# Four of seven products of a tile take the high and the low half of the weights in one matmul of 512 columns, and both late operands are made before the second product begins

## The chip, the cores and the metric

The kernel runs on one core of a Trainium2 chip. The time is device microseconds (us) of one execution, the median of three: 558.22 (557.73 to 558.32). Five engines run side by side, each with a queue of its own that is worked off in order: PE (TensorE, matmuls; its weight loads are shown as PEld), DVE (VectorE), ACT (ScalarE), POOL (GpSimd) and SP (here it issues DMAs). They wait for each other by semaphores.

## The reference, cut to what matters

```python
attn_out = _attn_ref(**attn_kwargs)              # causal softmax attention mixed with a memory read
x = attn_out.transpose(0, 2, 1, 3).reshape(2304, 512)
h = x @ w_in                                      # w_in 512 x 2048: the first product
r = np.maximum(h, 0.0)
g = s * (r * r) + b
return g @ w_out                                  # w_out 2048 x 512: the second product
```

## The kernel before

Until about 287 us the kernel computes attention, with most of the first product in its gaps. The rest of the first product runs to 373 us; beside it the weights `w_out` are loaded and made ready. The second product takes the rest. Everything in float32 is kept as two halves, H (rounded to fp32r) and L = x - H; a product of two such numbers is H\*BH + H\*BL + L\*BH, three matmuls into one PSUM tile.

The second product works on nine tiles of 256 rows (`t`). A tile is a 2 x 2 block of matrices a11, a12, a21, a22, and Winograd's scheme makes of eight block products seven, numbered 1 to 7 in `m`. Their operands are single blocks or sums of blocks; on the side of `w_out` the sums are made once (`t_u`, `split_u`, `late_b`), on the side of g for every tile (`operand`). A product has 1024 rows to sum over, eight steps `f`; its operand comes in two pieces `c` (four steps each). `SEQ` gives the order of the products in a tile, and operands are made two products ahead (`AH`), in eight buffers `xs`, so for four products. The operand's H is made by a cast on ACT (line 738), its L by a subtraction on DVE, or on POOL for products 1, 2 and 4 (line 739). The sums of blocks are made on DVE for products 5 and 6 (lines 735 and 737), on POOL for 7 and 3 (line 733). In the text, "6c1" is the second piece of product 6.

ACT also turns r into g for the next tile, in four pieces of four blocks each, a Square (line 712) and a scale with bias (line 713); `g_load` fetches the pieces from DRAM, into `w0L` and `w1L` in turn. `combine` adds the products into the output: one ACT copy (line 757) and seven DVE additions with one source in PSUM (lines 759 to 770) for a tile. PSUM tiles of a product are 128 x 256, eight of them.

Products 4 and 2 use the last weights to be ready, the "late" ones: H is cast from `late32` while the first product ends (line 682), L is subtracted on DVE in the first four products of tile 0 (line 684), since its place `w1H` is in use until the first product's last matmul.

A scheduler in the framework orders the queues by its own timeline, except where `pin` keeps an instruction in the program's order; so the order on an engine is not that of the code.

Of the kernel before, what the change touches and what calls it, by code (L numbers as in the profile page):

```python
# [165 lines left out]
def attention_moe_kernel(  # L166
# [456 lines left out]
    PL = {m: n for n, m in enumerate((1, 3, 5, 6, 7))}  # L623
    w2 = ctx.enter_context(tc.tile_pool(name="w2", bufs=1, side="right", reuse_waits="tile"))
    bHs, bLs = {}, {}
    RAW = [0, 1, 2, 3, 4, 5, 6, 7, 4, 5, 6, 7, 8, 6, 7, 8]
    NRAW = 4
    NEXT = {n: (n + 4,) for n in range(9)} | {3: (), 4: (7, 8)} | {10: (13,), 11: (14,), 12: (15,)}

    def load_u(n):  # L630

        t = w2.tile([128, DM, 2], U32, tag=f"row{RAW[n]}", name="raw")
        r = n // 2 + n % 2 * KF
        nc.sync.dma_start(t, words(w_out)[128 * r:128 * r + 128])
        st["u", n] = t

    def stage(i):

        if i == 0:
            return stg0  # L640
        if i < 4:
            k = 4 + 2 * ((i + 1) % 2)
            return [w2.tile([128, 4, NE], F32, tag=f"bl{k + j}", name="stg1") for j in range(2)]
        return stg[2 * (i % 2)], stg[2 * (i % 2) + 1]

    def conv_u(n):
        i, h = divmod(n, 2)
        if h == 0:
            st["b"] = stage(i)
        w, s = st["b"]  # L650
        conv64(st.pop(("u", n)), w[:, 2 * h:2 * h + 2].rearrange("p a b -> p (a b)"))
        if n in NEXT:
            for r in NEXT[n]:
                load_u(r)
        if h == 0:
            return
        later(2, t_u, i, w, s)
        later(4, split_u, i, w, s)

    def t_u(i, w, s):  # L660

        b12, b21, b22 = w[:, 1], w[:, 2], w[:, 3]
        t1, t2, t3 = s[:, 0], s[:, 1], s[:, 2]
        nc.vector.tensor_sub(t1, b12, w[:, 0])
        nc.vector.tensor_sub(t3, b22, b12)
        nc.vector.tensor_sub(t2, b22, t1)
        nc.vector.tensor_sub(late32[:, i, 0], t2, b21)

    def split_u(i, w, s):
        pin(nc.scalar.copy(late32[:, i, 1], w[:, 2]))  # L670
        bHs[i] = w2.tile([128, 5, NE], F32R, tag=f"row{i}", name="bH")
        bLs[i] = w2.tile([128, 5, NE], F32R, tag=f"bl{i}", name="bL")
        for x, a, n in ((w[:, 0:1], 0, 1), (w[:, 3:4], 1, 1), (s[:, 0:3], 2, 3)):
            L, H = bLs[i][:, a:a + n], bHs[i][:, a:a + n]
            pin(nc.scalar.copy(H, x))
            nc.vector.tensor_sub(L, x, H.bitcast(F32))

    def late_b(n, part):

        hs = slice(KF // 4 * n, KF // 4 * n + KF // 4)  # L680
        if part == 0:
            nc.scalar.copy(late[0][:, hs], late32[:, hs])
        else:
            nc.vector.tensor_sub(late[1][:, hs], late32[:, hs], late[0][:, hs].bitcast(F32))

    def b_op(m, f):
        if m in LATE:
            return [t[:, f, LATE.index(m)] for t in late]
        return bHs[f][:, PL[m]], bLs[f][:, PL[m]]

    NPT = NT // 256
# [25 lines left out]
    def operand(t, m, c):  # L717

        r = SRC[t % 2]
        f1 = slice(4 * c, 4 * c + 4)  # L720
        f2 = slice(KF + 4 * c, KF + 4 * c + 4)
        A = {11: r[:, f1, 0:128], 12: r[:, f2, 0:128], 21: r[:, f1, 128:256], 22: r[:, f2, 128:256]}
        if m == 7 and not SUM:
            both = w2.tile([128, 2, 4, 128], F32, tag="row8", name="sum")
            SUM.extend(both[:, i] for i in range(2))
        o = xpool.tile([128, 2, 4, 128], F32R, tag="xs", name="op")
        OPS[t, m, c] = o
        H, L = o[:, 0], o[:, 1]
        x = A[{1: 11, 7: 11, 5: 21, 6: 11, 3: 12, 2: 12, 4: 22}[m]]
        if m in (7, 3):  # L730
            y = x
            x = SUM[c]
            nc.gpsimd.tensor_sub(x, y, A[{7: 21, 3: 11}[m]])  # L733
        elif m == 5:
            nc.vector.tensor_add(x, x, A[22])
        elif m == 6:
            nc.vector.tensor_sub(x, A[21], x)  # L737
        nc.scalar.copy(H, x)  # L738
        (nc.gpsimd if m in ONPOOL else nc.vector).tensor_sub(L, x, H.bitcast(F32))  # L739

    def product(t, m):
        ps = ps_y.tile([128, NE], F32, tag="y", name="yps")
        for f in range(KF):
            o = OPS[t, m, f // 4]
            H, L = o[:, 0, f % 4], o[:, 1, f % 4]
            BH, BL = b_op(m, f)
            nc.tensor.matmul(ps, lhsT=H, rhs=BH, start=f == 0, stop=False)  # L747
# [24 lines left out]

    ONPOOL = (1, 2, 4)
# [9 lines left out]
    stg0 = [w2.tile([128, 4, NE], F32, tag=f"row{i}", name="stg0") for i in (8, 7)]
    for i in range(4, 7):
        w2.tile([128, 5, NE], F32, tag=f"row{i}", name="row")
    late32 = w2.tile([128, KF, 2, NE], F32, tag="late", name="late32")
    for i in range(KF):
        w2.tile([128, 5, NE], F32, tag=f"bl{i}", name="blr")

    def slot16(tag, dtype):  # L790
        return wpool.tile([128, KF, 2, NE], dtype, tag=tag, name=tag)
# [94 lines left out]
```

## Time and profile before

| | us |
|---|---|
| median of three runs | 558.22 |
| the profiled execution, its own time | 559.67 |
| its span, first to last instruction | 557.8 |
| PE busy | 542.8 |
| ACT busy | 397.4 |
| DVE busy | 359.4 |
| POOL busy | 302.5 |
| second product, first to last matmul start | 373.20 to 553.68 |

The profiled execution has 1.9 us around its span and is 1.45 us above the median. The granted clock of TensorE is 1.0 of full speed in all of the second product. A timeline row gives start and duration; rows of an engine overlap a little, so the pace of an engine is read from start to start. In brackets stands the time for which the engine sat idle before the row, and what ended it.

### The profile page before, as it was taken

How to read it: one execution, taken by the hardware profiler on the slowest of the kernel's cores; microseconds unless marked ns; L12 is line 12 of the kernel's file. 1: busy time of each engine (PE TensorE's matmuls, PEld its weight loads, DVE VectorE, ACT ScalarE, POOL GpSimd, SP SyncE). 2: the span in 40 equal slices, each digit the busy share in tenths (PEclk: the TensorE clock that was granted, in tenths of full speed). 3: DMA queues.
4: the chain of work that ended last, by engine and by line, in shares of the span. 5: the costliest groups of instructions: out<-in, count | busy, mean ns of one | idle time of the engine just before them, and what ended most of it. 6: DMA issues, size and time to landing. Idle time of an engine off the chain costs nothing.

```text
span 557.8 us, 12012 instructions
## 1 busy us (share of the span) xinstructions
PE 542.8 (97%) x4364; PEld 458.7 (82%) x4364; DVE 359.4 (64%) x885; ACT 397.4 (71%) x869; POOL 302.5 (54%) x327
## 2 busy tenths in 40 slices
PE   8997998999999999999999999999999999999997
PEld 6765766776777777777788888899999999999997
DVE  3999988999655554123108878336966786687562
ACT  5999877875968786337326568958779778877940
POOL 2788898768684595202200000325687678768750
PEclk8999899999999999999999999999999999999999
DMA  6546567664344343221137766447444435353101
GB/s 214 160 140 197 154 206 233 198 209 144 115 162 118 127 131 103 85 77 58 58 118 283 260 200 219 139 162 245 145 130 148 147 105 170 105 164 112 39 29 38
DMA packets 56666, 81.52 MB, mean 146 GB/s; under 512 B 7584, under 2 KB 39072, under 8 KB 56608
## 3 DMA queue, kind: packets, MB, share of 16 engines
q1 hardware_dynamic: 53616, 77.94, 43.6%
q10 hardware_dynamic: 2992, 2.82, 1.5%
q8 instruction: 34, 0.56, 0.4%
q14 instruction: 24, 0.20, 0.1%
HBM read 57.15 MB, written 23.59 MB: 145 GB/s over the span
## 4 chain that ended last, share of the span: by engine, by line
PE 80%; DVE 8%; POOL 5%; ACT 3%; issue 2%; DMA 1%; SPq 0%; POOLq 0%; DVEq 0%; ACTq 0%
PE yps L749 9%; PE yps L747 9%; PE yps L748 9%; PE tb L534 8%; PE sb L474 6%; PE tb L535 6%; PE tb L536 6%; PE sb L354 6%; PE hps L534 5%; PE hps L535 5%; PE hps L536 5%; PE tb L431 4%; POOL P L373 3%; DVE P L361 2%; ACT P L367 1%
## 5 line engine op out<-in xcount | busy, mean ns | idle before, releaser
L373 POOL TENSOR_SCALAR P<-P,sr,omg 128x192 f32<-128x192 f32 (+4 forms) x160 | 111.8, 712 | 63.2 <-DVE sr L405 42.7
L749 PE MATMUL yps<-bH,op 128*128 128x256 f32 x360 | 101.5, 282 | 0.7 <-DVE op L739 0.7
L747 PE MATMUL yps<-bH,op 128*128 128x256 f32 x360 | 101.3, 281 | 0.0
L748 PE MATMUL yps<-bL,op 128*128 128x256 f32 x360 | 101.3, 281 | 0.0
L367 ACT ACTIVATE P<-P,mn 128x64 f32<-128x64 f32 (+4 forms) x160 | 88.6, 564 | 13.7 <-DVE mn L361 13.3
L733 POOL TENSOR_TENSOR sum<-w0L 128x512 f32<-128x512 f32 x20 | 30.4, 1518 | 109.4 <-ACT w0L L713 87.9
L361 DVE CUSTOM_DVE_ANT_0 P<-sb,mask 128x64 f32<-128x64 f32 (+4 forms) x160 | 70.0, 482 | 28.8 <-PE sb L354 28.6
L749 PEld LDWEIGHTS yps<-bH,op 128*128 128x128 f32 x360 | 68.0, 189 | 1.0 <-DVE op L739 0.9
L748 PEld LDWEIGHTS yps<-bL,op 128*128 128x128 f32 x360 | 68.0, 189 | 0.0
L747 PEld LDWEIGHTS yps<-bH,op 128*128 128x128 f32 x360 | 67.9, 189 | 0.0
L354 PE MATMUL sb<-qk 64*128 64x288 f32 (+4 forms) x384 | 57.1, 418 | 3.9 <-DVE mn L361 2.6
L431 PEld LDWEIGHTS tb<-ident,P 64*128 64x128 f32 x928 | 37.7, 140 | 17.9 <-POOL P L373 6.8
L354 PEld LDWEIGHTS sb<-qk 64*128 64x128 f32 x384 | 36.4, 191 | 17.0 <-issue 8.6
L431 PE MATMUL tb<-ident,P 64*128 64x64 f32 x928 | 44.2, 231 | 4.2 <-POOL P L373 2.9
L441 ACT COPY pt<-tb 128x512 f32<-128x512 f32 x64 | 34.5, 596 | 18.7 <-PE tb L431 11.5
L739 POOL TENSOR_TENSOR op<-w0L,op 128x512 fp32r<-128x512 f32 x30 | 42.3, 1428 | 4.9 <-ACT op L738 4.7
L555 ACT ACTIVATE r<-tb 128x512 f32<-128x512 f32 x41 | 24.4, 594 | 26.9 <-PE tb L536 19.5
L733 POOL TENSOR_TENSOR sum<-w1L 128x512 f32<-128x512 f32 x16 | 24.4, 1528 | 32.1 <-DVE op L739 28.0
L738 ACT CAST op<-w0L 128x512 fp32r<-128x512 f32 x50 | 30.0, 616 | 16.1 <-DVE w0L L737 8.7
L534 PE MATMUL tb<-xs,w0H 128*128 128x512 f32 x96 | 40.7, 424 | 0.2 <-ACT F L443 0.2
L747 PE MATMUL yps<-w0H,op 128*128 128x256 f32 x144 | 40.8, 283 | 0.0
L748 PE MATMUL yps<-w1H,op 128*128 128x256 f32 x144 | 40.7, 283 | 0.0
(137 smaller groups left out, 1458.9 us busy)
## 6 DMA issues: line engine op xcount, KB each, us to landing
r_d<-r SPq DMA_DIRECT2D x41, 256.0 KB, 2.0
w0L<-r_d SPq DMA_DIRECT2D x20, 512.0 KB, 4.5
qk<-in_qk_t_dram SPq DMA_DIRECT2D x15, 576.0 KB, 4.4
raw<-in_moe_w_out_dram SPq DMA_DIRECT2D x16, 512.0 KB, 5.7
w1L<-r_d SPq DMA_DIRECT2D x16, 512.0 KB, 4.5
xa<-in_moe_w_in_dram SPq DMA_DIRECT2D x12, 512.0 KB, 4.5
r_d<-r SPq DMA_DIRECT2D x48, 128.0 KB, 1.8
qs<-in_q_rows_dram SPq DMA_DIRECT2D x15, 320.0 KB, 3.5
```

The costliest lines, as they stand in the source:

```text
L354: nc.tensor.matmul(SB[ps[j]][:, o:o + n], lhsT=qk[rs, 128 * i:128 * i + 128], rhs=qk[rs, S + 64 + c0:S + 64 + c0 + n], start=True, stop=Tr ...
L361: nc.vector.tensor_tensor_reduce(P[:, j, PB[i] + 64:PB[i] + 64 + n], SB[ps[j]][:, o:o + n], m, -SCALE, 3.0e38, ALU.add, ALU.min, mn[:, j, ...
L367: nc.scalar.activation(pt, pt, AF.Exp, scale=-1.0, bias=mn[:, j, i:i + 1], accum_out=sm[:, j, i, 0:1])
L373: nc.gpsimd.tensor_scalar(pt, pt, sr[:, j, i:i + 1], omg[:, h:h + 1], ALU.mult, ALU.mult)
L431: nc.tensor.transpose(TB[ps[h]][:, o[h]:o[h] + 64], P[rs, j, c:c + 128], ident[rs, rs], tile_position=(64 * h, 0))
L534: nc.tensor.matmul(ps, lhsT=wH[:, p, fs], rhs=xs[:, 0], start=p == 0, stop=False)
L535: nc.tensor.matmul(ps, lhsT=wH[:, p, fs], rhs=xs[:, 1], start=False, stop=False)
L536: nc.tensor.matmul(ps, lhsT=wL[:, p, fs], rhs=xs[:, 0], start=False, stop=p == NP - 1)
L733: nc.gpsimd.tensor_sub(x, y, A[{7: 21, 3: 11}[m]])
L747: nc.tensor.matmul(ps, lhsT=H, rhs=BH, start=f == 0, stop=False)
L748: nc.tensor.matmul(ps, lhsT=H, rhs=BL, start=False, stop=False)
L749: nc.tensor.matmul(ps, lhsT=L, rhs=BH, start=False, stop=f == KF - 1)
```

## The change

In `product`, the weights' H and L of a block now lie side by side (`RB`, and `late` with the same order inside), and products 1, 6, 3 and 2 (`WIDE`) multiply H with both in one matmul of 512 columns into a PSUM tile of 128 x 512, whose two halves are summed later. L\*BH goes into the first half. Products 5, 7 and 4 stay as they were, in half of such a tile. `combine` adds both halves, so it has eleven DVE additions for a tile instead of seven, beside the ACT copy.

The order of products is now 1, 5, 6, 7, 3, 2, 4. Product 5's sum a21 + a22 goes to a buffer of its own, `SUM`; product 6's operand is made in that same buffer, product 7's in place of a21, product 3's again in `SUM`. Before, 5 and 6 were made in place in the tile, and `SUM` held those of 7 and 3. Product 4 has the other sign in its weights.

`late_b` makes H and L together while the first product ends, into what were `w0H` and `w0L`; tile 0's pieces are then loaded where `late32` was, so `first_load` comes after `late_b`, five steps later than before. The rooms in which `w_out` is loaded and staged are cut differently; the work on them is the same.

```diff
-    SEQ = [1, 7, 5, 6, 3, 2, 4]
+    SEQ = [1, 5, 6, 7, 3, 2, 4]
...
-        nc.vector.tensor_sub(late32[:, i, 0], t2, b21)
+        nc.vector.tensor_sub(T32[i // 2][:, i % 2, 0], b21, t2)
...
-    def late_b(n, part):
-
-        hs = slice(KF // 4 * n, KF // 4 * n + KF // 4)
-        if part == 0:
-            nc.scalar.copy(late[0][:, hs], late32[:, hs])
-        else:
-            nc.vector.tensor_sub(late[1][:, hs], late32[:, hs], late[0][:, hs].bitcast(F32))
+    def late_b(n):
+
+        t = late[n // 2][:, 2 * (n % 2):2 * (n % 2) + 2]
+        H, L = t[:, :, :, 0], t[:, :, :, 1]
+        nc.scalar.copy(H, T32[n])
+        nc.vector.tensor_sub(L, T32[n], H.bitcast(F32))
...
-        x = A[{1: 11, 7: 11, 5: 21, 6: 11, 3: 12, 2: 12, 4: 22}[m]]
-        if m in (7, 3):
-            y = x
-            x = SUM[c]
-            nc.gpsimd.tensor_sub(x, y, A[{7: 21, 3: 11}[m]])
-        elif m == 5:
-            nc.vector.tensor_add(x, x, A[22])
+        x = {1: a11, 5: SUM[c], 6: SUM[c], 2: a12, 7: a21, 3: SUM[c], 4: a22}[m]
+        if m == 5:
+            nc.vector.tensor_add(x, a21, a22)
         elif m == 6:
-            nc.vector.tensor_sub(x, A[21], x)
+            nc.vector.tensor_sub(x, x, a11)
+        elif m == 7:
+            nc.gpsimd.tensor_sub(x, a11, x)
+        elif m == 3:
+            nc.gpsimd.tensor_sub(x, a12, x)
         nc.scalar.copy(H, x)
         (nc.gpsimd if m in ONPOOL else nc.vector).tensor_sub(L, x, H.bitcast(F32))
 
+    WIDE = (1, 6, 3, 2)
+
     def product(t, m):
-        ps = ps_y.tile([128, NE], F32, tag="y", name="yps")
+        OPS["ps", m] = tile = ps_y.tile([128, 2, NE], F32, tag="y", name="yps")
+        ps = tile[:, 0]
         for f in range(KF):
             o = OPS[t, m, f // 4]
             H, L = o[:, 0, f % 4], o[:, 1, f % 4]
-            BH, BL = b_op(m, f)
-            nc.tensor.matmul(ps, lhsT=H, rhs=BH, start=f == 0, stop=False)
-            nc.tensor.matmul(ps, lhsT=H, rhs=BL, start=False, stop=False)
-            nc.tensor.matmul(ps, lhsT=L, rhs=BH, start=False, stop=f == KF - 1)
+            B = b_op(m, f)
+            if m in WIDE:
+                nc.tensor.matmul(tile, lhsT=H, rhs=B, start=f == 0, stop=False)
+            else:
+                nc.tensor.matmul(ps, lhsT=H, rhs=B[:, 0], start=f == 0, stop=False)
+                nc.tensor.matmul(ps, lhsT=H, rhs=B[:, 1], start=False, stop=False)
+            nc.tensor.matmul(ps, lhsT=L, rhs=B[:, 0], start=False, stop=f == KF - 1)
...
+        def onto(y, x, n):
+            for h in range(2 if n in WIDE else 1):
+                nc.vector.tensor_add(y, y if h else x, OPS["ps", n][:, h])
+
         if m == 1:
-            nc.scalar.copy(U[0], ps[1])
+            nc.scalar.copy(U[0], OPS["ps", 1][:, 1])
+            nc.vector.tensor_add(U[0], U[0], OPS["ps", 1][:, 0])
         elif m == 6:
-            add(U[1], U[0], ps[6])
-            add(U[2], U[1], ps[7])
-            add(U[1], U[1], ps[5])
-            add(Y[:, 1, NE:], U[2], ps[5])
+            onto(U[1], U[0], 6)
+        elif m == 7:
+            onto(U[2], U[1], 7)
+            onto(U[1], U[1], 5)
+            onto(Y[:, 1, NE:], U[2], 5)
...
-            later(0, g_load, 0)
-            for i in range(4):
-                later(LT + i, g_make, 0, i)
-            for i in range(4):
-                later(max(LT + 4 + i, begin + CT[4 * i + 3] + 5 - clock[0]), late_b, i, 0)
             for i in range(4):
-                later(LT + 8 + i, operand, 0, SEQ[i // 2], i % 2)
+                later(max(i, begin + CT[4 * i + 3] + 5 - clock[0]), late_b, i)
+            later(LT, first_load)
+            for i in range(4):
+                later(LT + 6 + 2 * i, g_make, 0, i)
+            for i in range(4):
+                later(LT + 15 + i, operand, 0, SEQ[i // 2], i % 2)
...
-            if t == 0 and i < 4:
-                late_b(i, 1)
```

DVE in the second product, before, while the operands of the next tile are made: line 735 is product 5's sum (c0, then c1), 737 that of 6, 739 an operand's L (from `sum` product 7's), 761 to 767 additions for the output.

```order
L735 TENSOR_TENSOR w0L<-w0L 128x4x128
L761 TENSOR_TENSOR yu_4256<-yu_4256,yps 128x256
L762 TENSOR_TENSOR yu_4256<-yu_4256,yps 128x256
L735 TENSOR_TENSOR w0L<-w0L 128x4x128
L765 TENSOR_TENSOR yu_4256<-yu_4256,yps 128x256
L737 TENSOR_TENSOR w0L<-w0L 128x4x128
L739 TENSOR_TENSOR op<-sum,op 128x512 x2
L737 TENSOR_TENSOR w0L<-w0L 128x4x128
L739 TENSOR_TENSOR op<-w0L,op 128x512
```

The same place on DVE now: line 730 is product 5's sum, 738 an operand's L (the first two from `sum` are product 5's, the next two 6's, those from `src` 7's), 732 product 6's sum, 761 an addition for the output.

```order
L730 TENSOR_TENSOR sum<-src_3970,src_3972 128x512
L761 TENSOR_TENSOR yu_4241<-yu_4241,yps 128x256
L730 TENSOR_TENSOR sum<-src_3971,src_3973 128x512
L761 TENSOR_TENSOR yu_4241<-yu_4241,yps 128x256
L738 TENSOR_TENSOR op<-sum,op 128x512
L761 TENSOR_TENSOR yu_4241<-yu_4241,yps 128x256
L738 TENSOR_TENSOR op<-sum,op 128x512
L732 TENSOR_TENSOR sum<-sum,src_3970 128x512
L732 TENSOR_TENSOR sum<-sum,src_3971 128x512
L761 TENSOR_TENSOR yu_4241<-yu_4241,yps 128x256
L738 TENSOR_TENSOR op<-sum,op 128x512 x2
```

Product 6's sums moved behind the two L of product 5, which read the buffer that they overwrite; before, product 7's two L stood between them instead.

ACT at that place before: 712 and 713 are Square and scale of the next tile's pieces, 738 the casts of product 1 (from `w0L`, c0 and c1), of 7 (from `sum`), and of 5 and 6 (the last four).

```order
L712 ACTIVATE w0L<-w0L 128x1024
L713 ACTIVATE w0L<-w0L,b_sb,s_sb 128x1024
L738 CAST op<-w0L 128x512
L713 ACTIVATE w0L<-w0L,b_sb,s_sb 128x1024
L738 CAST op<-w0L 128x512
L738 CAST op<-sum 128x512 x2
L738 CAST op<-w0L 128x512 x4
L712 ACTIVATE w1L<-w1L 128x1024
```

ACT now (713 is the Square, 714 the scale, 737 the cast; the four from `sum` are 5c0, 5c1, 6c0, 6c1, the two behind them from `src` are 7's):

```order
L713 ACTIVATE src_3973<-src_3973 128x1024
L714 ACTIVATE src_3972<-src_3972,b_sb,s_sb 128x1024
L737 CAST op<-src_3970 128x512
L737 CAST op<-src_3971 128x512
L714 ACTIVATE src_3973<-src_3973,b_sb,s_sb 128x1024
L737 CAST op<-sum 128x512 x4
L737 CAST op<-src_3970 128x512
L737 CAST op<-src_3971 128x512
L713 ACTIVATE w1H<-w1H 128x1024
```

Product 7's two casts moved from ahead of those of 5 and 6 to behind them, and product 1's second cast to ahead of the last scale.

POOL at that place before (739 is an L, the first three here those of 2 and 4, the next two product 1's; 733 from `w0L` the sums of 3):

```order
L739 TENSOR_TENSOR op<-w1L,op 128x512 x3
L739 TENSOR_TENSOR op<-w0L,op 128x512 x2
L733 TENSOR_TENSOR sum<-w0L 128x512 x2
```

POOL now (738 is an L, of product 1; 734 product 7's sum in place of a21; 736 product 3's sum):

```order
L738 TENSOR_TENSOR op<-src_3970,op 128x512
L734 TENSOR_TENSOR src_3970<-src_3970 128x4x128
L738 TENSOR_TENSOR op<-src_3971,op 128x512
L734 TENSOR_TENSOR src_3971<-src_3971 128x4x128
L736 TENSOR_TENSOR sum<-src_3972,sum 128x512
```

Product 7's sums moved in between and behind the two L of product 1.

## Rows read from the trace of the kernel before

**Rows 1.** The page, busy time of each engine over the span.

```profile
PE 542.8 (97%) x4364; PEld 458.7 (82%) x4364; DVE 359.4 (64%) x885; ACT 397.4 (71%) x869; POOL 302.5 (54%) x327
```

**Rows 2.** Waits from 372 us on: total us, times, longest.

```profile
ACT op L738 <- DVE w1L L737: 8.9, 6, 2.3
...
PE yps L749 <- DVE op L739: 0.7, 1, 0.7
```

**Rows 3.** PE timeline, first product: start, duration; 8, 12 and 4 matmuls apart.

```profile
308.68 0.39 PE L535 MATMUL hps<-xs,w0H 128*128 128x512 f32 x1
...
310.50 0.28 PE L534 MATMUL hps<-x,w0H 128*128 128x256 f32 x1
...
311.93 0.40 PE L534 MATMUL hps<-xs,w0H 128*128 128x512 f32 x1
...
312.86 0.39 PE L535 MATMUL hps<-xs,w0H 128*128 128x512 f32 x1
```

**Rows 4.** PE timeline, first and last of the second product's 1512 matmuls.

```profile
373.20 0.28 PE L747 MATMUL yps<-bH,op 128*128 128x256 f32 x1
...
553.68 0.28 PE L749 MATMUL yps<-w0H,op 128*128 128x256 f32 x1
```

**Rows 5.** ACT timeline, one tile of the second product.

```profile
456.46 0.62 ACT L738 CAST op<-w0L 128x512 fp32r<-128x512 f32 x1 [2.28 <-DVE w0L L737]
...
458.45 1.24 ACT L713 ACTIVATE w1L<-w1L,b_sb,s_sb 128x1024 f32<-128x1024 f32 x1
459.60 0.35 ACT L757 COPY yu<-yps 128x256 f32<-128x256 f32 x1
459.85 0.62 ACT L738 CAST op<-sum 128x512 fp32r<-128x512 f32 x1
460.37 1.06 ACT L712 ACTIVATE w1L<-w1L 128x1024 f32<-128x1024 f32 x1
461.33 0.61 ACT L738 CAST op<-w0L 128x512 fp32r<-128x512 f32 x1
...
467.58 0.61 ACT L738 CAST op<-w1L 128x512 fp32r<-128x512 f32 x1
...
472.92 0.63 ACT L738 CAST op<-w1L 128x512 fp32r<-128x512 f32 x1 [0.91 <-DVE w1L L737]
475.82 0.62 ACT L738 CAST op<-w1L 128x512 fp32r<-128x512 f32 x1 [2.28 <-DVE w1L L737]
```

**Rows 6.** DVE timeline in the same tile.

```profile
467.78 1.63 DVE L735 TENSOR_TENSOR w1L<-w1L 128x512 f32<-128x512 f32 x1 [1.27 <-ACT w1L L713]
469.33 0.41 DVE L761 TENSOR_TENSOR yu<-yu,yps 128x256 f32<-128x256 f32 x1
...
469.99 1.13 DVE L735 TENSOR_TENSOR w1L<-w1L 128x512 f32<-128x512 f32 x1
...
471.38 1.45 DVE L737 TENSOR_TENSOR w1L<-w1L 128x512 f32<-128x512 f32 x1
472.75 1.28 DVE L739 TENSOR_TENSOR op<-sum,op 128x512 fp32r<-128x512 f32 x2
473.96 1.78 DVE L737 TENSOR_TENSOR w1L<-w1L 128x512 f32<-128x512 f32 x1
```

**Rows 7.** POOL timeline in the same tile.

```profile
465.04 3.83 POOL L739 TENSOR_TENSOR op<-w0L,op 128x512 fp32r<-128x512 f32 x3
468.81 3.48 POOL L739 TENSOR_TENSOR op<-w1L,op 128x512 fp32r<-128x512 f32 x2
473.51 1.68 POOL L733 TENSOR_TENSOR sum<-w1L 128x512 f32<-128x512 f32 x1 [1.23 <-DVE op L739]
```

**Rows 8.** ACT timeline, the casts of product 1 for tile 1.

```profile
389.93 1.12 ACT L738 CAST op<-w1L 128x512 fp32r<-128x512 f32 x2
```

**Rows 9.** DVE timeline, first sum for tile 0, and the late weights' L.

```profile
359.21 1.44 DVE L735 TENSOR_TENSOR w0L<-w0L 128x512 f32<-128x512 f32 x1 [7.62 <-ACT w0L L713]
...
376.66 4.63 DVE L684 TENSOR_TENSOR w1H<-late,w0H 128x1024 fp32r<-128x1024 f32 x4
```

More of the change, by code (lines that the diff above doesn't have):

```diff
@@ L623, in attention_moe_kernel, with room @@
     PL = {m: n for n, m in enumerate((1, 3, 5, 6, 7))}
+    STG = {0: 7, 1: 6, 2: 5, 3: 7}
+    NEXT = {n: (n + 4,) for n in range(6)} | {7: (10, 11)} | {n: (n + 4,) for n in range(8, 12)}
     w2 = ctx.enter_context(tc.tile_pool(name="w2", bufs=1, side="right", reuse_waits="tile"))
[L625 to L628, printed above, removed]
+    RB = {}
+    T32 = [w2.tile([128, 2, 2, NE], F32, tag=f"late{i}", name="late32") for i in range(KF // 2)]
+    def room(k, dtype, name):
+        t = w2.tile([128, 2, 1280], dtype, tag=f"rb{k}", name=name)
+        return [t[:, h, :1024] for h in range(2)]
     def load_u(n):
-        t = w2.tile([128, DM, 2], U32, tag=f"row{RAW[n]}", name="raw")
+        if n % 2 == 0:
+            st["raw"] = room(n // 2, U32, "raw")
+        t = st["raw"][n % 2].rearrange("p (c b) -> p c b", b=2)
         r = n // 2 + n % 2 * KF
@@ L637, in stage @@
     def stage(i):
[L639 to L643, printed above, removed]
+        if i in STG:
+            return [t.rearrange("p (a e) -> p a e", e=NE) for t in room(STG[i], F32, "stg")]
         return stg[2 * (i % 2)], stg[2 * (i % 2) + 1]
@@ L651, in conv_u @@
         conv64(st.pop(("u", n)), w[:, 2 * h:2 * h + 2].rearrange("p a b -> p (a b)"))
-        if n in NEXT:
-            for r in NEXT[n]:
-                load_u(r)
+        for r in NEXT.get(n, ()):
+            load_u(r)
         if h == 0:
@@ L694, in g_load @@
     def g_load(t):
-        for f in range(0, NF, 4):
+        for n in range(4):
             c = 256 * (t % 2)
-            nc.sync.dma_start(SRC[t % 2][:, f:f + 4], r_d[t // 2][:, f:f + 4, c:c + 256])
+            nc.sync.dma_start(SRC[t % 2][n], r_d[t // 2][:, 4 * n:4 * n + 4, c:c + 256])
     def put_out(t, h, cs, y):
@@ L719, in operand @@
         r = SRC[t % 2]
[L720 to L723, printed above, removed]
+        a11, a12, a21, a22 = r[c][:, :, 0:128], r[2 + c][:, :, 0:128], r[c][:, :, 128:256], r[2 + c][:, :, 128:256]
+        if not SUM:
             both = w2.tile([128, 2, 4, 128], F32, tag="row8", name="sum")
@@ L779, in attention_moe_kernel, with first_load, slot16 @@
     SUM = []
-    LT = 2
-    for i in range(NRAW):
-        load_u(i)
[L783 to L791, printed above, removed]
+    LT = 5
+    def first_load():
+        SRC.append([w2.tile([128, 4, 256], F32, tag=f"late{i}", name="src0") for i in range(4)])
+        g_load(0)
+    for i in range(4):
+        load_u(i)
+    for i in range(2, KF):
+        w2.tile([128, 2, 1280], F32, tag=f"rb{i}", name="rb")
+    def slot16(tag, dtype, shape):
+        return wpool.tile([128, *shape], dtype, tag=tag, name=tag)
     begin = clock[0]
@@ L811, in attention_moe_kernel @@
     flush()
-    late.append(slot16("w1H", F32R))
-    SRC.append(slot16("w1L", F32).rearrange("p f a (b n) -> p (f a b) n", n=256))
+    both = slot16("w1H", F32, [4, 4, 256])
+    SRC.append([both[:, n] for n in range(4)])
     YU = []
-    for t in (x4pool.tile([128, 2048], F32, tag="x4", name="yu0"), w2.tile([128, 2048], F32, tag="late", name="yu1")):
+    for t in (x4pool.tile([128, 2048], F32, tag="x4", name="yu0"), wpool.tile([128, 2048], F32, tag="w1L", name="yu1")):
         YU.append((t[:, :1024].rearrange("p (j e) -> p j e", j=2),
-                   [t[:, 1024 + NE * k:1024 + NE * k + NE] for k in range(3)]))
+                   [t[:, 1024 + NE * k:1024 + NE * k + NE] for k in range(4)]))
     p3.close()
```

25 lines of the change are left out of this document (10 added, 15 removed).

## The prediction

> **What bounds the kernel now.** I read the page first: PE is busy 97% of the span, the next engine 71% [rows 1], so PE's stream sets the time. Then the waits of the second product: PE waited once, 0.7 us, for an operand's L on DVE; ACT waited far more, for product 6's sums on DVE [rows 2]. So there is a second loop below PE's, and the question is how far below. PE's own pace: the second product's 1512 matmuls start between 373.20 and 553.68 [rows 4], 0.1194 us each with the wait in it. A tile of 168 matmuls takes 168 x 0.119 = 20.0 us.
>
> The second loop shows in ACT's rows [rows 5]. The last cast of product 6 starts at 456.46 after an idle 2.28, and again at 475.82: 19.36 us later, less than PE's 20.0. Both times ACT had waited for DVE, and between the casts of product 1 at 467.58 and of 6c1 at 475.82 stand 0.91 and 2.28 of idle time. ACT was thus bound by its own work and DVE, behind PE's need, and catching up by 0.6 us for a tile. The operands' loop needs 19.36 us; PE hides it with 0.6 to spare.
>
> **The change part by part.**
>
> *512 columns.* Four products of eight steps in nine tiles: 288 pairs of matmuls of 256 columns become one of 512. From the first product, where both widths follow each other: 512 columns take (310.50 - 308.68)/8 = 0.2275 us, 256 take (311.93 - 310.50)/12 = 0.119 [rows 3]. A pair costs 0.238, so 0.0105 is saved, 288 x 0.0105 = 3.0 us. The low end is the slower 512 of (312.86 - 311.93)/4 = 0.2325 [rows 3]: 1.6 us. I take 3.0, since most rows show it. PE's tile becomes 4 x 8 x (0.2275 + 0.119) + 3 x 24 x 0.119 = 19.66 us.
>
> Against this stands a rule of the Trainium skill ("TensorE: Matmul & The Clock Gate", Back-to-back issue gap): a warm matmul of N columns follows the one before after N/2.4 + 2.5 ns. By it a pair would cost 218.4 ns, one of 512 215.8, and the saving would be an estimated 0.7 us. The rows have about 14 ns over N/2.4 at 512 columns and 12 at 256, so the trace speaks for 3.0.
>
> *Late operands.* DVE's four subtractions (4.63 us at 376.66, [rows 9]) leave tile 0. Their new place has cover: DVE stood idle 7.62 us before tile 0's first sum at 359.21 [rows 9], 14 us ahead of the second product. The loads behind them on SP come later, with the stores of the first product queued behind; I cost that at nothing, at up to 3 us if tile 0's operands miss 373.20. What they give back in tile 0 is no more than PE's one wait, 0.7 us.
>
> *Four more additions in a tile* on DVE. Such a row has 0.41 us (a slot of 0.33) and is not stretched while POOL runs: 469.33 lies inside POOL's 468.81 + 3.48 [rows 6, 7]. Two of them lie in the chain below, beside POOL operations that DVE would wait for anyway: nothing; uncovered, 2 x 0.33 in seven tiles, 4.6 us.
>
> *The operands' new order.* This decides. DVE's subtractions and sums with two sources in SBUF and POOL's operations take turns: with a POOL operation between, DVE's ends lie 1.71 us apart (469.41, 471.12, 472.83; 474.03 to 475.74), without one 0.60 (472.83 to 474.03) [rows 6, 7]. POOL alone needs 3.83/3 = 1.28 [rows 7]. ACT's slots, start to start [rows 5]: cast 0.52, Square 0.96, scale 1.15, copy 0.25.
>
> Now the chain, from T = 0, the start of product 1's first cast (467.58 in the rows). Before, 6c1's cast started at T + 8.24, and inside that time ACT also did product 7's two casts. In the new order ACT does casts 1c0 and 1c1, then the last scale, which begins at 1.04 and has its result at 1.04 + 1.24 = 2.3. DVE then asks for 5c1's sum. POOL began with 1c0's L when its cast was done, at 0.6, and goes straight on to 7c0's sum, whose only condition (5c0's sum) is met: 0.6 + 2 x 1.28 = 3.2. So 5c1's sum ends at 3.8; with 1c1's L on POOL between, 5c0's L ends at 5.5; with 7c1's sum between, 5c1's L at 7.2. Only then may product 6 be made in the same buffer: its sums end at 7.8 and 8.4, and 6c1's cast starts at 8.5. The wait is as long as before, but nearly empty. Behind it ACT had 19.36 - 8.24 - 0.52 = 10.6 us of work to the next T; now product 7's two casts are added, 11.64. The loop is 8.5 + 0.52 + 11.64 = 20.6 us, 0.94 above PE's new 19.66. The operands become the bound.
>
> *The sum.* In tile 1, T was at 389.93 [rows 8]; the work ahead of it on ACT is much the same, so I keep 389.9. 6c1's L ends about 10.7 after T: cast from 8.5 to 9.1, then one POOL operation (3c0's sum, free since 6c0's L at 9.0) and the L, 9.0 + 1.71. For tile 8 that is 389.9 + 7 x 20.6 + 10.7 = 544.8. In the first tiles DVE has one more L or addition ahead of the last sum of 6, about 1 us together: 545.8. PE then has half of product 6 (1.39) and 7, 3, 2 and 4 (2.86 + 2.77 + 2.77 + 2.86): 558.4, against 553.8 before (the last start and 0.12). The tail behind it, 4 us to the end of the span, stays. So the span grows by 4.6, from 557.8 to 562.4; the profiled execution would go from 559.67 to 564.3, and the median, which lies 1.45 lower, to 562.8.
>
> Bounds: half a POOL turn (1.11/2 = 0.55) less or more in each of seven loops is 3.9 us: 558.9 to 566.7.
>
> **The rivals.**
>
> *Operands keep up; faster.* If the chain is shorter by one POOL turn of 1.11 (DVE's sum of 5c1 or an L of 5 gets ahead of 7's sums), the loop is 19.5, below 19.66. Then PE's stream sets the time again. Tile 1 is late by 389.9 + 10.7 - (373.2 + 19.66 + 7.03) = 0.7, as before, and the saving stays whole: 558.2 - 3.0 = 555.2; with tile 0's wait gone too 554.5, with the low end for 512 columns 556.6. It decides at a loop of 19.66. For it: ACT has only 16 us of slots in a tile. Against it: in every row DVE waited its turn [rows 6], and POOL's 7c0 stands directly behind 1c0's L.
>
> *About even.* With a loop between 19.8 and 20.1, what PE saves is given back to the operands: 557.1 to 559.3. It needs half of that POOL turn to go.
>
> *The change doesn't do what it says:* a matmul of 512 columns might cost as much as two of 256, the weights' load being paid either way. But before, too, every matmul has a load of its own [rows 1], and 512 still has 0.2275 [rows 3]. With operands keeping up that would be 557.5 to 558.2. By the skill's gap rule above, an estimate of 557.5. It is a small part of the even case.
>
> **How the numbers follow.** Forecast (operands bound, 559 to 567): 0.63. Even: 0.12. Faster (554.4 to 557): 0.25. The time is that of the forecast, 562.8. The range for 8 in 10 has to take in the faster case, which has more than 0.2: 554.4 to 566.7. About 0.2% or 1.1 us is what a measurement of this kernel can tell from no change; the three chances are those of the cases.
>
> **What would show it.** Right: PE waits in nearly every tile from 1 on, up to 1 us each, for an L on DVE of product 6 or 7; ACT's product 1 casts lie 20.3 to 20.9 us apart; ACT idles some 5 us in a tile, in one stretch ahead of 6c1's cast, and not for PE. 512-column rows of the second product are 0.227 to 0.233 before the next start. Wrong: PE without waits and tiles of 19.7 us (the operands keep up); ACT's tile below 19.7; or a wait at 373 us for tile 0's operands, which I took as covered. A loop that is right with a first T earlier or later than 389.9 shifts the time by as much.

## The result and the profile after

The changed kernel takes 563.41 us (median of six, 562.44 to 564.92), the kernel before beside it 558.70 (557.73 to 561.11): the ratio is 1.008, with an interval of 1.0056 to 1.0107. It is slower by 4.7 us, where 4.6 were forecast. The profiled execution took 564.47 us, with a span of 562.7. (One execution of a later experiment, e10, took 753.14 us at a granted clock of 0.654 and is left out of its numbers.)

The page's lines of busy time and of clock, to be held against [rows 1]:

```profile
span 562.7 us, 11448 instructions
PE 545.0 (97%) x4076; PEld 445.3 (79%) x4076; DVE 378.9 (67%) x921; ACT 397.8 (71%) x869; POOL 302.2 (54%) x327
PEclk9899999999999999999999999999999999999999
```

PE has 288 matmuls fewer and is busy longer; nothing on this page tells why. The matmul rows do: first and last matmul of the second product, as [rows 4] have them for before.

```profile
374.80 0.40 PE L750 MATMUL yps<-rb,op 128*128 128x512 f32 x1
...
558.84 0.28 PE L754 MATMUL yps<-w0L,op 128*128 128x256 f32 x1
```

184.04 us lie between them, against 180.48 before. Taken per tile (every 136th matmul's start), PE needs 19.70 and 19.79 us in tiles 0 and 1, then 20.05, 21.01, and 20.5 to 20.9 from there on. It started below the old pace of 19.95 and lost it on the way. The waits of the second product (line waited, releaser: us in all, times, longest), to be held against [rows 2]:

```profile
ACT op L737 <- DVE sum L732: 29.4, 11, 3.4
ACT op L737 <- DVE sum L730: 8.7, 8, 1.1
PEld yps L754 <- DVE op L738: 4.7, 8, 1.0
PE yps L754 <- DVE op L738: 2.5, 5, 0.8
PEld yps L754 <- POOL op L738: 1.0, 2, 0.5
PE yps L754 <- POOL op L738: 0.5, 2, 0.3
```

PE's one wait has become a wait in nearly every tile, for an operand's L (line 738 is now the subtraction, 737 the cast, 730 and 732 the sums of 5 and 6). Two of them, with the matmuls around:

```profile
481.93 0.50 PE L750 MATMUL yps<-rb,op 128*128 128x512 f32 x1
482.74 0.39 PE L754 MATMUL yps<-rb,op 128*128 128x256 f32 x1 [0.30 <-DVE op L738]
482.96 0.40 PE L750 MATMUL yps<-rb,op 128*128 128x512 f32 x1
483.20 0.28 PE L754 MATMUL yps<-rb,op 128*128 128x256 f32 x1
483.31 0.40 PE L750 MATMUL yps<-rb,op 128*128 128x512 f32 x1
...
520.23 0.39 PE L754 MATMUL yps<-rb,op 128*128 128x256 f32 x1 [0.56 <-DVE op L738]
```

From 481.93 to 482.74 it is 0.81 us instead of 0.24, so PE lost 0.57, more than the 0.30 in brackets: the rows of PE overlap, and a bracket counts only from the end of the row before. So waits of PE are better read from start to start. Summed over all starts that come more than 20 ns late, PE lost 5.9 us.

ACT's loop, to be held against [rows 5]. The cast at 481.26 is 6c0's; the one before it came at 460.60, the one after at 501.91.

```profile
473.37 1.12 ACT L737 CAST op<-w1H 128x512 fp32r<-128x512 f32 x2
474.40 1.24 ACT L714 ACTIVATE w1H<-w1H,b_sb,s_sb 128x1024 f32<-128x1024 f32 x1
475.54 0.60 ACT L737 CAST op<-sum 128x512 fp32r<-128x512 f32 x1
477.24 0.62 ACT L737 CAST op<-sum 128x512 fp32r<-128x512 f32 x1 [1.09 <-DVE sum L730]
481.26 1.22 ACT L737 CAST op<-sum 128x512 fp32r<-128x512 f32 x2 [3.40 <-DVE sum L732]
482.39 1.14 ACT L737 CAST op<-w1H 128x512 fp32r<-128x512 f32 x2
...
484.39 0.35 ACT L764 COPY yu<-yps 128x256 f32<-128x256 f32 x1
...
494.03 0.60 ACT L737 CAST op<-src 128x512 fp32r<-128x512 f32 x1
```

From T (473.37) to the next T (494.03) it takes 20.66 us, and so from there on in every tile. The wait is nearly empty and product 7's casts (482.39) stand behind it, as the prediction had it. DVE and POOL inside that wait, to be held against [rows 6, 7]:

```profile
475.67 1.47 DVE L730 TENSOR_TENSOR sum<-w1H 128x512 f32<-128x512 f32 x1 [1.15 <-ACT w1H L714]
477.40 1.45 DVE L738 TENSOR_TENSOR op<-sum,op 128x512 fp32r<-128x512 f32 x1
479.10 1.45 DVE L738 TENSOR_TENSOR op<-sum,op 128x512 fp32r<-128x512 f32 x1
480.47 1.28 DVE L732 TENSOR_TENSOR sum<-sum,w1H 128x512 f32<-128x512 f32 x2
...
474.05 2.55 POOL L738 TENSOR_TENSOR op<-w1H,op 128x512 fp32r<-128x512 f32 x2 [1.13 <-ACT op L737]
476.56 3.45 POOL L734 TENSOR_TENSOR w1H<-w1H 128x512 f32<-128x512 f32 x2
```

As long as POOL works, a DVE operation with both sources in SBUF takes 1.45 us; after POOL's end at 480.01 two take 1.28 together.

For the experiments the loop is cut in two at the end of the last scale (475.64 here): **the chain**, from there to the start of 6c0's cast, 5.62 us, and **ACT's stretch** from that cast to the next last scale's end, 15.04. In a tile past the first three:

| kernel | median us, ratio to before | second product | loop | stretch (idle in it) | chain |
|---|---|---|---|---|---|
| after | 563.41, 1.008 | 184.04 | 20.66 | 15.04 (0) | 5.62 |
| e6: order 1, 5, 7, 6 | 562.15, 1.006 | 184.99 | 20.70 | 15.70 (1.55) | 5.00 |
| e8: copy on DVE | 561.54, 1.004 | 182.04 | 20.62 | 14.63 (0.26) | 5.98 |
| e9: rows made earlier | 572.74, 1.024 | 193.37 | 21.86 | 15.06 (1.05) | 6.80 |
| e7: lows of 1 on DVE | 557.38, 0.997 | 178.17 | 20.2, at last 20.0 | 15.05 to 15.4 | 5.2 to 4.6 |
| e11: sums of 7 on DVE | 558.42, 0.999 | 178.87 | 19.3 to 21.1 | 14.5 to 15.6 | 4.5 to 5.9 |

The kernels with the old order make 6's two casts some 3 us apart, so this cut does not suit them, and only their loops compare: e3 20.05, e10 20.83, e5 19.35 until PE holds it up at 19.95.

### The profile page after: what moved, and what is told of

Same layout as the page of the kernel before. It is cut to its first block, busy times and chain, and to the rows that moved or that the text cites. A ratio compares the mean times of both kernels' runs of the same rounds, so it can differ in the third digit from the quotient of the medians.

```text
span 562.7 us, 11448 instructions
## 1 busy us (share of the span) xinstructions
PE 545.0 (97%) x4076; PEld 445.3 (79%) x4076; DVE 378.9 (67%) x921; ACT 397.8 (71%) x869; POOL 302.2 (54%) x327
## 4 chain that ended last, share of the span: by engine, by line
PE 64%; DVE 16%; ACT 11%; POOL 4%; issue 2%; DMA 2%; SPq 0%; DVEq 0%; ACTq 0%; POOLq 0%
PE tb L534 8%; PE sb L474 6%; PE tb L535 6%; PE tb L536 6%; DVE op L738 6%; PE sb L354 5%; PE hps L534 5%; PE hps L535 5%; PE hps L536 5%; PE yps L754 4%; PE yps L750 4%; PE tb L431 4%; POOL P L373 3%; ACT src L714 3%; DVE yu L761 2%
## 5 line engine op out<-in xcount | busy, mean ns | idle before, releaser
L754 PE MATMUL yps<-rb,op 128*128 128x256 f32 x360 | 101.7, 284 | 3.1 <-DVE op L738 2.5
L738 POOL TENSOR_TENSOR op<-src,op 128x512 fp32r<-128x512 f32 x30 | 40.7, 1375 | 105.4 <-ACT op L737 105.4
L750 PE MATMUL yps<-rb,op 128*128 128x512 f32 x216 | 77.6, 396 | 0.0
L754 PEld LDWEIGHTS yps<-rb,op 128*128 128x128 f32 x360 | 67.8, 188 | 6.0 <-DVE op L738 4.7
L737 ACT CAST op<-sum 128x512 fp32r<-128x512 f32 x54 | 33.2, 616 | 40.9 <-DVE sum L732 29.4
L738 DVE TENSOR_TENSOR op<-sum,op 128x512 fp32r<-128x512 f32 x54 | 51.0, 959 | 8.7 <-ACT op L737 8.5
L750 PEld LDWEIGHTS yps<-rb,op 128*128 128x128 f32 x216 | 40.6, 188 | 8.1
L761 DVE TENSOR_TENSOR yu<-yu,yps 128x256 f32<-128x256 f32 x90 | 36.5, 414 | 15.3 <-PE yps L754 13.7
L555 ACT ACTIVATE r<-tb 128x512 f32<-128x512 f32 x41 | 24.4, 595 | 26.9 <-PE tb L536 19.5
L534 PE MATMUL tb<-xs,w0H 128*128 128x512 f32 x96 | 40.6, 423 | 0.2 <-ACT F L443 0.2
L753 PE MATMUL yps<-rb,op 128*128 128x256 f32 x144 | 40.5, 281 | 0.0
L752 PE MATMUL yps<-rb,op 128*128 128x256 f32 x144 | 40.5, 281 | 0.0
L738 POOL TENSOR_TENSOR op<-w1H,op 128x512 fp32r<-128x512 f32 x24 | 32.0, 1354 | 14.7 <-ACT op L737 14.7
L535 PE MATMUL tb<-xs,w0H 128*128 128x512 f32 x96 | 37.6, 392 | 0.0
```

The source lines that it names most:

```text
L534: nc.tensor.matmul(ps, lhsT=wH[:, p, fs], rhs=xs[:, 0], start=p == 0, stop=False)
L535: nc.tensor.matmul(ps, lhsT=wH[:, p, fs], rhs=xs[:, 1], start=False, stop=False)
L750: nc.tensor.matmul(tile, lhsT=H, rhs=B, start=f == 0, stop=False)
L754: nc.tensor.matmul(ps, lhsT=L, rhs=B[:, 0], start=False, stop=f == KF - 1)
L761: nc.vector.tensor_add(y, y if h else x, OPS["ps", n][:, h])
```

## The experiments

**Two more profiles.** Of the 4.9 us between the spans, 1.6 lie ahead of the second product, where both programs run the same instructions.

> The kernel before, unchanged, profiled once more. In the two profiles at hand the second stage (first hps matmul) begins at 287.28 us before and at 288.88 us after, though the instructions up to there are the same; that is 1.6 us of the 4.9 us by which the spans differ. Theory V (it varies from execution to execution): the first hps matmul comes anywhere from 287 to 289 us in this run and in the next, with no rule between the two kernels. Rival P (the changed program itself starts later, by where its tiles lie): 287.0 to 287.6 us here, 288.6 to 289.2 us with the changed kernel.

> The changed kernel, profiled once more. Theory V: first hps matmul anywhere from 287 to 289 us. Rival P: 288.6 to 289.2 us. Both: the second product, from its first to its last yps matmul, takes 184.0 us within 0.5, and the sum's copies on ACT (one per tile) stand 20.6 to 20.7 us apart in the later tiles, as in the profile of after.

The first hps matmul came at 288.67 us before and at 287.07 after, the other way round than in the first two profiles. In all fourteen profiles of this study it lies between 286.80 and 289.01 us, so theory V holds: this is a difference between executions. The second product took 184.02 us again; the kernel before took 179.40 this time:

```profile
374.59 0.28 PE L747 MATMUL yps<-bH,op 128*128 128x256 f32 x1
...
553.99 0.28 PE L749 MATMUL yps<-w0H,op 128*128 128x256 f32 x1
```

The wait of [rows 2], which with its after-effect cost 1.1 us, was not there. So the change costs 4.6 us in the second product against an execution without that wait, nearly the whole difference of the medians (4.7).

**The old order, and the narrow matmuls.**

```diff
-    SEQ = [1, 5, 6, 7, 3, 2, 4]
+    SEQ = [1, 7, 5, 6, 3, 2, 4]
...
-        x = {1: a11, 5: SUM[c], 6: SUM[c], 2: a12, 7: a21, 3: SUM[c], 4: a22}[m]
+        x = {1: a11, 7: SUM[c], 5: a21, 6: a11, 3: SUM[c], 2: a12, 4: a22}[m]
```

This restores the old buffers together with the order, and the place where the products are added up (not shown).

> The changed kernel with the operand order of before (1, 7, 5, 6, 3, 2, 4, product 7's sums in the spare room, 5 and 6 made in place); the 512-column matmuls, the four more additions and the early late operands stay. Theory O (the new operand order makes the operands the bound): the sum's copies on ACT come 19.4 to 19.9 us apart instead of 20.66, TensorE has under 1.5 us of waits in the second product instead of 5.9, and the second product takes 178.5 to 180.5 us instead of 184.0; the time is 555.5 to 558.5 us, 0.995 to 1.000 of before. Rival W (the wide matmuls, their additions or the early late operands cost the time): the second product stays at 183 us or more and the time at 562 us or more.

The time was 557.65 us, 0.996 of before (0.995 to 0.9976), and PE did not wait once in the second product. Theory O holds. First and last matmul are 178.08 us apart, and 6c0's casts 20.05:

```profile
373.62 0.40 PE L750 MATMUL yps<-rb,op 128*128 128x512 f32 x1
...
551.70 0.28 PE L754 MATMUL yps<-w0L,op 128*128 128x256 f32 x1
```

The loop is a little longer than expected, and longer than PE's tile, 19.81 us; the second product is a little shorter than expected. It still did not show, for the operands start with a lead: eight loops lose 8 x 0.24 = 1.9 us of it.

```diff
-    WIDE = (1, 6, 3, 2)
+    WIDE = ()
...
-            nc.scalar.copy(U[0], OPS["ps", 1][:, 1])
-            nc.vector.tensor_add(U[0], U[0], OPS["ps", 1][:, 0])
+            nc.scalar.copy(U[0], OPS["ps", 1][:, 0])
```

> The changed kernel with all 24 matmuls per four rows at 256 columns, and without the four additions that the wide ones need; the new operand order and the early late operands stay. Theory O: the loop of the operands does not see the width of the matmuls, so the copies still come 20.4 to 20.7 us apart and the time stays at 562 to 564 us, 1.006 to 1.010 of before. Rival W: back to 558 to 559.5 us.

564.62 us, 1.009 (1.0071 to 1.0101); the loop was 20.8, the second product 185.75 us. Time and loop lie just above what was expected. Rival W falls: with the new order the kernel is slow without wide matmuls and without their additions, by a little more even.

> The changed kernel with the operand order of before and all matmuls at 256 columns (no extra additions): of the change only the rooms and the early late operands are left. Beside the run with the old order and wide matmuls (second product 178.08 us without a wait on TensorE, 19.81 us a tile) this measures what the wide matmuls give. Theory: 19.95 us a tile, as before, so 179.4 us for the second product, 4.4 ns for each of 288 wide matmuls; the time is 558.5 to 559.5 us, 0.998 to 1.001 of before. Rival (the 10.5 ns a matmul of the prediction): 20.1 us a tile, 181 us, 560.5 us.

This is e3 with the edit of e4. 558.97 us, a ratio of 1.000 (0.9991 to 1.001), 179.41 us without a wait, 19.95 us a tile. So the new rooms and the early late operands cost and give nothing that can be measured, and the wide matmuls give 0.14 us a tile: 4.4 ns each, 1.3 us in all. The four kernels together are a square: the wide matmuls are worth 1.3 us with the old order (558.97 to 557.65) and 1.2 with the new one (564.62 to 563.41, which the spread of those runs does not tell from nothing); the order costs 5.7 us with either width.

**What in the order costs it.** Product 7's casts back inside the wait:

```diff
-    SEQ = [1, 5, 6, 7, 3, 2, 4]
+    SEQ = [1, 5, 7, 6, 3, 2, 4]
...
             onto(U[1], U[0], 6)
-        elif m == 7:
             onto(U[2], U[1], 7)
```

> The changed kernel with product 7 between 5 and 6 (1, 5, 7, 6, 3, 2, 4); what each operand is made of, and on which engine, stays. So product 7's two casts on ACT (1.04 us) stand inside the wait for 6's sums and no longer behind it. Theory L (the loop is the way from product 1's first cast to 6's second cast, 8.4 to 8.5 us, and then all of ACT's work that stands behind it): the copies come 19.5 to 19.8 us apart instead of 20.66, TensorE's waits fall from 5.9 us to under 2, the second product takes 178 to 180.5 us, the time is 557 to 559.5 us. Rival B (what binds is 5's sums and lows themselves, 5.5 us after product 1's cast, wherever 7's casts stand): copies 20.4 us or more apart, time 562 us or more.

The forecast failed: 562.15 us (1.0045 to 1.0075), loop 20.70. ACT's work in the stretch did fall by 0.9 us, but 1.55 us of new waits came into it. DVE shows where they are from:

```profile
477.16 3.15 DVE L738 TENSOR_TENSOR op<-sum,op 128x512 fp32r<-128x512 f32 x2
480.23 0.68 DVE L732 TENSOR_TENSOR sum<-sum,w1H 128x512 f32<-128x512 f32 x1
480.83 0.68 DVE L738 TENSOR_TENSOR op<-w1H,op 128x512 fp32r<-128x512 f32 x1
481.43 0.41 DVE L761 TENSOR_TENSOR yu<-yu,yps 128x256 f32<-128x256 f32 x1
481.76 0.68 DVE L732 TENSOR_TENSOR sum<-sum,w1H 128x512 f32<-128x512 f32 x1
...
476.31 3.44 POOL L734 TENSOR_TENSOR w1H<-w1H 128x512 f32<-128x512 f32 x2
```

5's lows still take 1.6 us each beside POOL's sums of 7, and 6's second sum (481.76) now stands behind 7c0's low (480.83). Where 7's casts stand does not decide; what DVE and POOL do ahead of 6 does.

```diff
-    ONPOOL = (1, 2, 4)
+    ONPOOL = (2, 4)
```

> The changed kernel with product 1's two lows on DVE instead of POOL, the order kept. DVE has two more operations a tile (0.6 to 0.75 us each), POOL two fewer beside 5's sums. Theory T (DVE's chain is slow because POOL's lows run beside it and the two take turns: 1.47 us where DVE alone takes 0.6 to 0.75): from product 1's first cast to 6's second sum it takes 6 to 7.5 us instead of 8.4, the copies come 19.8 us or less apart, the second product takes 178 to 180 us, the time is 556.5 to 559 us. Rival Q (the length of DVE's own queue is what counts): 8.4 us or more, copies 20.6 us or more apart, 562.5 us or more.

557.38 us, 0.997 (0.9954 to 0.9978), second product 178.17. DVE is busier (385.8 us against 378.9), and yet the kernel is as fast as with the old order. 6c0's cast twice, and POOL beside it:

```profile
475.08 1.22 ACT L737 CAST op<-sum 128x512 fp32r<-128x512 f32 x2 [2.87 <-DVE sum L732]
...
494.99 0.62 ACT L737 CAST op<-sum 128x512 fp32r<-128x512 f32 x1 [2.53 <-DVE sum L732]
...
469.28 1.68 POOL L734 TENSOR_TENSOR w1H<-w1H 128x512 f32<-128x512 f32 x1 [2.18 <-DVE sum L730]
471.58 1.30 POOL L734 TENSOR_TENSOR w1H<-w1H 128x512 f32<-128x512 f32 x1 [0.63 <-DVE sum L730]
```

Q falls; T holds for the sign and the time, not for the sizes. From product 1's first cast to 6's it took 6.5 to 6.7 us in tiles 1 to 3 (7.3 in after), as T had it, but 7.5 to 8.6 in the later ones (7.9 in after): from tile 5 on the scheduler had a scale between product 1's two casts. The chain fell by 0.4 to 1.0 us, and the loop to 19.9 to 20.2, not under 19.8. That was enough only because of the lead: PE lost 0.1 us in all, in the last tile.

```diff
-            nc.scalar.copy(U[0], OPS["ps", 1][:, 1])
+            nc.vector.tensor_copy(U[0], OPS["ps", 1][:, 1])
```

> The changed kernel with one operation of ACT moved: the copy of product 1's second half (0.35 us, 11 us after product 1's first cast, so outside the wait) goes to DVE. Theory L (each microsecond of ACT outside the wait counts in full in the loop): the copies' places, now on DVE, and product 1's casts come 0.25 to 0.35 us closer, 20.3 to 20.4 us; the second product 1.5 to 2.5 us shorter (181.5 to 182.5), the time 560.5 to 562 us. Rival (the loop is bound by DVE, which has one operation more now): 20.66 us or more, 563 us or more.

561.54 us (1.0027 to 1.0056): in the expected range, but not by the expected way. The loop stayed at 20.62, with less in ACT's stretch and 0.36 more in the chain. The 2 us came from the first tiles: T to T took 20.78, 20.73 and 20.65 us there, against 21.92, 20.99 and 21.26. Why the first loops got shorter was not settled; the scheduler had moved scales and casts on ACT against each other as well. As a measure of ACT's share in the loop this run is inconclusive.

```diff
-    AH, GM = 2, 1
+    AH, GM = 2, 0
```

> The changed kernel with the next tile's squares and scales one product earlier in the program (GM = 0), the operand order kept. On ACT the last scale then stands ahead of product 1's two casts, no longer behind them. Theory S (the loop is ACT's work from 6's first cast to the last scale's end, 15.04 us, and then 5.62 us until 6's first sum: 5's sums need the last row group, so the chain starts at that scale): 1.04 us of casts leave the first stretch for the wait, so the loop is 14.0 + 5.6 to 6.0 = 19.6 to 20.0 us; TensorE waits under 1 us, the second product takes 178 to 179 us, the time is 556.5 to 558.5 us. Rival C (the chain starts at product 1's casts, by POOL's lows and 7's sums, wherever the scale stands): 20.5 to 20.7 us, 562 us or more.

A plain miss: 572.74 us, 1.024 (1.0217 to 1.026). ACT's work in the stretch fell to 14.0 us as theory S had it, but the chain grew to 6.8, and 1.05 of idle time came between 6's casts. POOL shows what the forecast had left out:

```profile
475.32 1.30 POOL L738 TENSOR_TENSOR op<-src,op 128x512 fp32r<-128x512 f32 x1 [0.58 <-ACT op L737]
476.57 1.31 POOL L734 TENSOR_TENSOR w1H<-w1H 128x512 f32<-128x512 f32 x1
477.83 1.75 POOL L738 TENSOR_TENSOR op<-src,op 128x512 fp32r<-128x512 f32 x1
479.55 1.74 POOL L738 TENSOR_TENSOR op<-w1H,op 128x512 fp32r<-128x512 f32 x1
481.25 1.74 POOL L734 TENSOR_TENSOR w1H<-w1H 128x512 f32<-128x512 f32 x1
482.96 1.71 POOL L738 TENSOR_TENSOR op<-w1H,op 128x512 fp32r<-128x512 f32 x1
...
481.76 3.45 DVE L732 TENSOR_TENSOR sum<-sum,w1H 128x512 f32<-128x512 f32 x2
```

With the casts of product 4 of the tile before now later on ACT, its lows (the rows from `src`) came later on POOL too, and so beside the chain. 6's two sums, 1.28 us without POOL, took 3.45. So ACT had less to do, DVE the same, and the chain got 1.2 us longer with POOL's work beside it: the clearest sign of what sets its length.

```diff
-            nc.gpsimd.tensor_sub(x, a11, x)
+            nc.vector.tensor_sub(x, a11, x)
```

> The changed kernel, its order kept, with product 7's two sums on DVE instead of POOL. DVE gets two operations more into its chain (0.6 to 0.75 us each where no POOL operation lies between), POOL has only product 1's two lows left beside it. Theory T (POOL operations beside the chain stretch it: from the last scale's end to 6's first sum 5.6 us with four of them, 5.1 with two): 3.8 to 4.8 us here although DVE does more, so a loop of 15.04 + 3.8 to 4.8 = 18.9 to 19.9 us; TensorE has no waits worth naming, 19.8 us a tile, second product 178.1 to 178.5, time 556.5 to 558.5 us. Rival Q (DVE's own load counts): 6.0 us or more from the scale to the sum, copies 20.7 us or more apart, 562 us or more.

The edit is to product 7's sum. 558.42 us, 0.9985 (0.9971 to 0.9998), 178.87 us for the second product, 0.9 of it waits. The time is T's, and Q falls again: two operations more on DVE, and 5 us less. The sizes are not T's. The chain was 4.5 to 5.9 us instead of 3.8 to 4.8; the scheduler had put one or both of 7's sums ahead of 5's lows and moved the ACT copy in among the casts of 5 and 6, where in the last two tiles it waited 1.2 and 2.0 us for PE.

**All products wide.** With the old order, and with e11's edit:

```diff
-    WIDE = (1, 6, 3, 2)
+    WIDE = (1, 7, 5, 6, 3, 2, 4)
```

> The kernel with the old order and wide matmuls (557.65 us), and now all seven products wide; four more additions a tile on DVE (products 7 and 4 one each, 5 two). Theory A (each wide matmul gives 4.4 ns and the operands, 20.05 us a tile there against TensorE's 19.81, still have lead enough): 19.70 us a tile, the second product 177.1 us, the time 556.5 to 557 us. Rival D (additions on DVE lengthen the operands' loop, as from 19.36 to 20.05 us with the first five, so now to 20.6 us, and the lead runs out): TensorE waits 2 to 5 us, the time is 559 to 562 us.

> The same with all seven products wide. If theory T holds and the loop is under 19.9 us, there is room for the four more additions: TensorE 19.70 us a tile without waits, second product 177.1 to 177.5, time 556 to 557.5 us, about 0.995 of before and under the best so far (557.4). Rival D (the additions lengthen the operands' loop by 0.14 to 0.2 us each and the lead runs out, as with the old order and all wide): loop 20.3 us or more, waits in the last tiles, 558.5 to 562 us.

Both came out at rival D's times: 563.27 us (1.0061 to 1.0092) and 560.55 (1.0016 to 1.004). In e10 PE ran four tiles at 19.5 to 19.7 us, as theory A had it, and then was held to the loop of 20.83; the copies on ACT, and DVE from the first to the second sum of 6 (L734):

```profile
481.89 0.35 ACT L764 COPY yu<-yps 128x256 f32<-128x256 f32 x1
...
502.72 0.35 ACT L764 COPY yu<-yps 128x256 f32<-128x256 f32 x1
...
473.32 1.77 DVE L734 TENSOR_TENSOR w1H<-w1H 128x512 f32<-128x512 f32 x1 [1.19 <-POOL op L738]
475.01 0.74 DVE L761 TENSOR_TENSOR yu<-yu,yps 128x256 f32<-128x256 f32 x2
...
476.87 0.41 DVE L761 TENSOR_TENSOR yu<-yu,yps 128x256 f32<-128x256 f32 x1
477.20 1.46 DVE L734 TENSOR_TENSOR w1H<-w1H 128x512 f32<-128x512 f32 x1
```

With the old order the loop is 19.35 us without extra additions (e5), 20.05 with four (e3), 20.83 with eight (e10): 0.7 to 0.8 us for four, 0.2 for one that takes 0.41. From the last scale's end to 6's second cast it takes 6.47, 7.18 and 7.97 us, and from there to the next scale's end 12.88 in all three: the whole lengthening lies in the chain, where no addition stands between 6's two sums in e5, one in e3 and three in e10. The widths changed with the additions in these runs and were not tested apart from them. PE gains 0.14 and 0.13 for that. In e12 D's mechanism is not shown: PE kept to 19.5 to 19.7 us for four tiles and then needed 19.8 to 21.2, but in the last four ACT's copy stood among the casts of 5 and 6 and waited 0.4 to 2.0 us for PE. The fastest kernels of this study are e7 and e3, 0.997 and 0.996 of before, not to be told apart; both are faster than the kernel before and the changed one.

## Why the prediction was right, and where it was not

**The mechanism was right.** The operands became the bound, and the reckoning of the chain stands row for row. Against T the prediction had 5c1's sum end at 3.8, 5c0's L at 5.5, 5c1's L at 7.2, 6's sums at 7.8 and 8.4; the rows of DVE give (477.14, 478.85, 480.55, 481.75 less 473.37) 3.8, 5.5, 7.2 and 8.4. The loop was 20.6 by the sum and 20.66 in the trace. Only ACT's idle time, forecast at some 5 us in one stretch, came as 4.5 in two (1.09 and 3.40). e3 and e4 show that the order, with the buffers that go with it, does it, and not the width; order and buffers were not tested apart. e7 and e9 show that POOL's operations beside the chain stretch it.

**The sum was right by partly cancelling errors.** T of tile 8 was forecast at 535.1 and came at 535.36. But the second product began 1.6 us later in that execution, so counted from its start T was 1.3 us early. T of tile 1 came at 388.54, 13.7 us after the start instead of 16.7; the loops of the first three tiles, 21.92, 20.99 and 21.26, gave 1.4 of these 3 us back, being 2.4 us over three of 20.6 where "about 1 us together" was forecast. Steady loops could be forecast to 0.1 us; the first tiles could not.

Most of the 3 us was the execution from which T was read. There ACT stood idle for a DMA just ahead of tile 0's casts; in the second profile of the kernel before T comes 14.25 us after the start. The idle row of the first, and T in the second:

```profile
374.53 0.39 ACT L541 ACTIVATE r<-hps 128x256 f32<-128x256 f32 x1 [1.89 <-DMA r_d<-r]
...
388.84 1.13 ACT L738 CAST op<-w1L 128x512 fp32r<-128x512 f32 x2
```

So the size was in part luck. By the forecast the second product takes 185.1 us, and it took 184.0; without the wait of that execution the kernel before takes 179.4, and not the 180.5 from which the forecast counted. Two errors of 1.1 us cancel in the 4.6.

**512 columns: the mis-sized term.** 3.0 us were taken, at the pace of the first product; 1.3 came (e5 against e3), below even the low end of 1.6. In the second product the row after a wide one starts 0.23 to 0.24 us behind it (482.96 to 483.20), where 0.2275 was taken from [rows 3]; the slower 0.2325 there was the better guide. By the gap rule of the Trainium skill ("TensorE: Matmul & The Clock Gate", Back-to-back issue gap) an estimated 0.7 had been held against this; the measurement lies between the two. That section gives the formula for a single matmul by itself, and says that a stream of weight loads and matmuls keeps another pace; this kernel is such a stream. Since PE did not set the end, the error cost the forecast nothing. It would have cost 1.7 us in the rival case.

**Late operands: right.** e5 is at 1.000, and tile 0's first matmul follows 0.23 us after the first product's last (374.57 and 374.80). But the 0.7 us that were to be won were those of a wait in one execution (in tile 1): the second profile of before has none.

**The point from which it decides: wrong.** The prediction set it at a loop of 19.66 us, with tile 1 already late. In e3 (20.05) and e7 (20.0 to 20.2) the loop was longer than PE's tile, and the kernel still ran at PE's pace. The step missing in the sum is the lead: nine tiles can lose some 3 us of it before PE notices (e7: 6c0's cast in tile 1 at 393.04, in tile 8 at 534.99, which is 3.35 us more than 7 x 19.80; it was just at the edge). The "about even" case, a loop of 19.8 to 20.1, would have come out faster.

**Which operand PE waits for: half right.** 6c1's L in the middle tiles (482.74, 9.4 after T), and in tiles 3 and 4 also 1c1's, which POOL makes (436.43, 457.69); in the last ones it was 5c0's L, 5.5 after T (499.56, 520.23, 540.91 less 494.03, 514.68, 535.36). The prediction looked only at the operand that came last.

**The additions: right here, wrong in general.** They cost nothing with the new order (e4), but with the old one four of them, with their wide matmuls, lengthen the loop by 0.7 to 0.8 us (e10, e3, e5).

## What to carry to other kernels

Look for the second loop, not for the second busiest engine: an engine at 71% with a wait in every round can become the bound by a change of order that adds no work to it. Write such a chain down from the rows, and count whose operations run beside it on the engine that takes turns with it; an operation moved to the busier of the two engines can make the kernel faster. And ask how long a loop may be too long before its lead is used up: over nine rounds some 3 us of lead hid up to 0.5 us a round, and by the same arithmetic it would not have lasted for twice as many.

## What the runs showed of the hardware

A PE wait costs more than its gap. After each L that came late, the matmul has 0.39 us instead of 0.28, and the next one starts 0.22 after it instead of 0.12 (482.74 to 482.96, against 483.20 to 483.31): 0.1 us for each of a dozen waits, 1.2 of the 5.9 us.

The same instructions, from the start to the second stage, took 286.80 to 289.01 us from execution to execution. Two profiles alone would have put 1.6 us of that on the change.
